# A fused sigmoid-attention and SiLU-MLP kernel rewritten: attention of four heads in 64x64 quadrants, the second matmul by seven products of halves, all engines in one planned order

## The chip, the cores and the metric

The kernel runs on one core of one Trainium2 chip. The metric is the device time of one execution in microseconds (us). Before the change it was 448.87 us, the median of 2 runs (448.57 to 449.17). The span that a profile shows, from the first to the last instruction, is about 2 us shorter than the time of the same run. A *granted clock* is the share of full speed that the matrix engine's clock had in a stretch, as the trace records it. PSUM is the memory into which the matrix engine writes its sums, in banks; SBUF is the memory that holds the operands. DVE, ACT and POOL are VectorE, ScalarE and GpSimd, PE is the matrix engine.

## The reference, cut to what matters

```python
batch, n_heads, seq, head_dim = (8, 12, 448, 64)          # q, k, v, float32
n_tokens, d_model, d_ff = (3584, 768, 2048)               # 3584 = 8 * 448, 768 = 12 * 64

def _attn_ref(q, k, v):
    scores = np.matmul(q, k.transpose(0, 1, 3, 2)) / np.sqrt(64) - np.log(448)
    return np.matmul(1.0 / (1.0 + np.exp(-scores)), v)    # a sigmoid, no row sums

def _moe_ref(x, w_in, w_out):                             # x: heads side by side, 3584 x 768
    h = x @ w_in                                          # "first GEMM"
    return (h / (1.0 + np.exp(-h))) @ w_out               # "second GEMM"
```

## The kernel before

Scores are computed transposed, for a pair of heads at a time, 112 keys per step. Two matmuls, one per head, use the upper and the lower half of the array's rows. The value products use the left and the right half of its columns. ScalarE applies the sigmoid as it empties PSUM.

```python
    def scores(b, hp, c0, c1):
        # ... (tiles)
        for c in range(c0, c1):                           # 4 chunks of 112 keys
            psc = ps_sc.tile([P, 2, 512], F32, ...)
            for j in range(2):                            # 2 heads: 64 rows of the array each
                nc.tensor.matmul(psc[:CP, j, :S],
                    kT[j * D : (j + 1) * D, gi * NCH + c, :],
                    qT[j * D : (j + 1) * D, gi * NCH : (gi + 1) * NCH, :], start=True, stop=True)
            nc.scalar.activation(attnT[:, :, c, :], psc[:CP, :, :S], AF.Sigmoid, ...)

    def values(b, hp):
        # ...
        for c in range(NCH):
            for j in range(2):                            # 2 heads: 64 columns of the array each
                nc.tensor.matmul(pav[j * D : (j + 1) * D, :S],
                    v16[:, 2 * hp + j, c, :], attnT[:, j, c, :], ...)

    def gemm_stream():                                    # both GEMMs, cut into pieces
        for m in range(B // 2):
            for b in (2 * m, 2 * m + 1):
                for fc in range(NFC):                     # first GEMM: 6 matmuls of 448 columns
                    h_unit(b, fc)
                    yield T_H
            for g in range(2 * S // P):
                # ...
                for nh in range(2):
                    for fc in range(NFC):                 # second GEMM: 16 matmuls of 384 columns
                        nc.tensor.matmul(po[:, :NO2], gTs[m][:, fc, g * P : (g + 1) * P],
                                         w_out_sb[:, fc, nh * NO2 : (nh + 1) * NO2], ...)
                # ... scale on VectorE, store
```

Batch 0 runs its attention alone. From batch 1 on, pieces of attention ("visits") are put between pieces of the GEMMs. Of batches 1 to 7, q and k are cast on GpSimd and transposed by DMA; batch 0's are transposed on the matrix engine. Only the instruction orders of the matrix engine (PE) and of GpSimd (POOL) are fixed by hand.

## Time and profile before

| what | number |
|---|---|
| time | 448.87 us |
| PE busy, share of the span | 408.7 us, 91% |
| VectorE (DVE) busy | 173.9 us, 39% |
| ScalarE (ACT) busy | 246.1 us, 55% |
| first matmul of the second GEMM | 118.3 us |

The page of the kernel before, its busy totals and then busy tenths, granted PE clock and DMA share in 40 slices of 11.2 us:

```profile
PE 408.7 (91%) x2480; PEld 197.4 (44%) x2480; DVE 173.9 (39%) x251; ACT 246.1 (55%) x322; POOL 66.3 (15%) x113
...
PE   0477839999999999999999999999999999999996
...
PEclk9998959999999999999999999999999999999999
DMA  9999999999991994089214932071011010000211
```

After about seven slices PE is full to the end. Before that it is not, and there the DMA row is full (it stays full for five slices more). So there are two regimes: a start that waits for data, then a long stretch in which only PE time counts.

The price of PE work is read from the timeline of the kernel before (columns: start, length, engine, line, operation, output<-inputs, shape, count):

```profile
201.61 1.30 PE L201 MATMUL ph_6_1897<-xT_1363,w_in_sb 128*128 128x448 f16 x6
202.84 0.40 PE L161 MATMUL psc_1_2_1907<-qT_0_1280,kT_0_1285 64*112 64x448 f16 x2
203.07 0.35 PE L161 MATMUL psc_1_3_1911<-qT_0_1280,kT_0_1285 64*112 64x448 f16 x2
203.35 1.31 PE L201 MATMUL ph_7_1915<-xT_1363,w_in_sb 128*128 128x448 f16 x6
204.50 1.30 PE L201 MATMUL ph_8_1925<-xT_1363,w_in_sb 128*128 128x448 f16 x6
```

Read starts, not lengths: the lengths of 1.30 us overlap starts that are 1.15 us apart, because matmuls are pipelined. Groups of six without a visit are 1.14 to 1.15 us apart, 0.19 us per matmul; with a visit of two score steps they are 1.74 us apart. The visit costs 0.60 us, of which the two steps are 0.38 and changing to attention's tiling and back is 0.22. Groups of 16 second-GEMM matmuls start 2.60 us apart, 0.1625 us each.

### The profile page before, as it was taken

To read this page: it belongs to the slowest core of one execution; us is meant where nothing else is said; L and a number is where in the kernel's file an instruction comes from. 1 tells how busy PE (TensorE), PEld (TensorE's weight loads), DVE (VectorE), ACT (ScalarE), POOL (GpSimd) and SP (SyncE) were. 2 spreads that over 40 slices of the span, in tenths; PEclk is the share of its full clock that TensorE was granted. 3 is DMA by queue.
4 is the path that set the end of the run, shared out by engine and by line. 5 is a ranking of instruction groups with operands and counts; after the bars stand their busy time and mean duration, and the time that the engine had idled before them with its cause. 6 is when DMAs were issued, how large, how long until landed. Compare 5 with 4: busy or idle time off the path is not lost.

```text
span 447.5 us, 6131 instructions
## 1 busy us (share of the span) xinstructions
PE 408.7 (91%) x2480; PEld 197.4 (44%) x2480; DVE 173.9 (39%) x251; ACT 246.1 (55%) x322; POOL 66.3 (15%) x113
## 2 busy tenths in 40 slices
PE   0477839999999999999999999999999999999996
PEld 0122314344455554444455544444554544455663
DVE  1133314546423235465432335555423235553221
ACT  1356918977644447787545547777555457542000
POOL 1236123262101500051004200130000000000000
PEclk9998959999999999999999999999999999999999
DMA  9999999999991994089214932071011010000211
GB/s 204 221 184 202 244 167 245 264 170 210 202 279 56 214 244 117 1 133 258 42 70 81 285 105 58 2 109 36 5 67 72 35 72 1 0 1 17 90 72 71
DMA packets 81468, 54.86 MB, mean 123 GB/s; under 512 B 40480, under 2 KB 77856, under 8 KB 81440
## 3 DMA queue, kind: packets, MB, share of 16 engines
q1 hardware_dynamic: 65312, 42.67, 40.6%
q0 software_dynamic: 16128, 11.80, 18.5%
q8 instruction: 19, 0.31, 0.3%
q14 instruction: 9, 0.07, 0.0%
HBM read 45.61 MB, written 11.01 MB: 127 GB/s over the span
## 4 chain that ended last, share of the span: by engine, by line
PE 72%; DMA 5%; POOL 1%; DVE 0%; issue 0%
DMA w_out_sb<-in_moe_w_out_dram 5%; PE po_6_1_3490 L228 1%; PE po_5_1_3425 L228 1%; PE po_4_1_3360 L228 1%; PE po_3_1_3302 L228 1%; PE po_3_0_3276 L228 1%; PE po_2_1_3237 L228 1%; PE po_0_1_3093 L228 1%; PE po_0_0_3075 L228 1%; PE po_6_0_2482 L228 1%; PE po_5_0_2403 L228 1%; PE po_4_0_2337 L228 1%; PE po_3_1_2309 L228 1%; PE po_2_0_2210 L228 1%; PE po_1_1_2171 L228 1%; PE po_1_0_2145 L228 1%
## 5 line engine op out<-in xcount | busy, mean ns | idle before, releaser
L201 PEld LDWEIGHTS <-w_in_sb 128*128 128x128 f16 x768 | 71.3, 98 | 79.8 <-issue 19.1
L228 PEld LDWEIGHTS <-gTr_436 128*128 128x128 f16 x224 | 20.9, 98 | 17.8 <-issue 4.9
L228 PEld LDWEIGHTS <-gTr_1537 128*128 128x128 f16 x224 | 20.9, 98 | 17.2 <-issue 4.2
L228 PEld LDWEIGHTS <-gTr_2538 128*128 128x128 f16 x224 | 20.9, 98 | 17.1 <-issue 4.2
L228 PEld LDWEIGHTS <-gTr_3517 128*128 128x128 f16 x224 | 21.9, 98 | 14.5
L131 PE MATMUL ptr_0_k<-ident,x1k_0_109 112*128 112x112 f16 x4 | 0.6, 291 | 11.2 <-POOL x1k_0_109 L125 11.2
L168 ACT ACTIVATE attnT_0_117<-psc_0_0_118,bias_s 112x896 f16<-112x896 f32 x1 | 1.0, 1008 | 15.3 <-PE psc_0_0_118 L161 15.3
L180 PE MATMUL pav_0_485<-attnT_0_427,v_1_399 112*64 112x448 f16 x8 | 1.7, 581 | 7.4 <-DMA v_1_399<-in_v_dram 7.4
L180 PEld LDWEIGHTS <-v_1_399 112*64 112x64 f16 x48 | 2.4, 117 | 10.1 <-DMA v_1_399<-in_v_dram 7.7
L143 POOL DMA_DIRECT2D v_5_1778<-in_v_dram x1 | 0.9, 939 | 36.1 <-PE pav_5_1789 L180 36.1
L143 POOL DMA_DIRECT2D v_6_2279<-in_v_dram x1 | 0.9, 935 | 35.5 <-PE pav_5_2290 L180 35.5
L143 POOL DMA_DIRECT2D v_7_2769<-in_v_dram x1 | 0.9, 935 | 35.0 <-PE pav_5_2780 L180 35.0
L209 ACT ACTIVATE tsig_3_502<-ph_3_495 128x448 f16<-128x448 f32 x1 | 0.5, 544 | 9.7 <-PE ph_3_495 L201 9.7
L180 PEld LDWEIGHTS <-v_0_86 112*64 112x64 f16 x48 | 3.0, 142 | 5.7 <-issue 5.4
L131 PEld LDWEIGHTS <-x1k_0_109 112*128 112x128 f16 x4 | 0.3, 129 | 11.4 <-POOL x1k_0_109 L125 11.4
L188 DVE TENSOR_SCALAR xT_484<-pav_0_485 128x448 f16<-128x448 f32 x1 | 1.1, 1150 | 8.5 <-PE pav_0_485 L180 8.5
L131 PE MATMUL ptr_0_q<-ident,x1q_0_100 112*128 112x112 f16 x4 | 0.6, 294 | 4.1 <-DVE x1q_0_100 L125 4.1
L143 POOL DMA_DIRECT2D v_4_1287<-in_v_dram x1 | 1.0, 955 | 21.2 <-PE pav_5_1298 L180 21.2
L180 PEld LDWEIGHTS <-v_7_2769 112*64 112x64 f16 x48 | 2.2, 109 | 3.0 <-issue 2.1
L180 PEld LDWEIGHTS <-v_3_783 112*64 112x64 f16 x48 | 2.2, 109 | 2.9 <-issue 2.0
L180 PEld LDWEIGHTS <-v_5_1778 112*64 112x64 f16 x48 | 2.2, 109 | 2.9 <-issue 2.0
L180 PEld LDWEIGHTS <-v_2_425 112*64 112x64 f16 x48 | 2.2, 109 | 2.9 <-issue 2.0
(1101 smaller groups left out, 983.6 us busy)
## 6 DMA issues: line engine op xcount, KB each, us to landing
w_in_sb<-in_moe_w_in_dram POOLq DMA_DIRECT2D x4, 768.0 KB, 11.0
w_out_sb<-in_moe_w_out_dram POOLq DMA_DIRECT2D x4, 768.0 KB, 15.6
v_0_86<-in_v_dram POOLq DMA_DIRECT2D x1, 672.0 KB, 12.9
v_1_399<-in_v_dram POOLq DMA_DIRECT2D x1, 672.0 KB, 19.7
v_2_425<-in_v_dram POOLq DMA_DIRECT2D x1, 672.0 KB, 14.9
v_3_783<-in_v_dram POOLq DMA_DIRECT2D x1, 672.0 KB, 7.1
v_4_1287<-in_v_dram POOLq DMA_DIRECT2D x1, 672.0 KB, 7.9
v_5_1778<-in_v_dram POOLq DMA_DIRECT2D x1, 672.0 KB, 7.3
```

Of the source, the lines that this page charges most:

```text
L131: nc.tensor.transpose(ptr[:, c * CP : (c + 1) * CP], x1[:, c].rearrange("p j d -> p (j d)"), ident[:CP, :CP],)
L143: nc.gpsimd.dma_start(v16.rearrange("p h c d -> p h (c d)"), v[b].rearrange("h (p c) d -> p h (c d)", c=NCH),)
L168: nc.scalar.activation(attnT[:, :, c, :], psc[:CP, :, :S], AF.Sigmoid, bias=bias_s[:CP], scale=QKSCALE)
L180: nc.tensor.matmul(pav[j * D : (j + 1) * D, :S], v16[:, 2 * hp + j, c, :], attnT[:, j, c, :], start=(c == 0), stop=(c == NCH - 1),)
L188: nc.vector.tensor_scalar_mul(xTs[b][:, hp, :].rearrange("e (p c) -> e c p", c=NCH), pav[:, :S].rearrange("e (c p) -> e c p", c=NCH), SX,)
L201: nc.tensor.matmul(ph[:, :S], w_in_sb[:, cc, fc * P : (fc + 1) * P], xTs[b][:, cc, :], start=(cc == 0), stop=(cc == NCC - 1),)
L209: nc.scalar.activation(tsig, ph[:, :S], AF.Sigmoid, bias=0.0, scale=ISX)
L228: nc.tensor.matmul(po[:, :NO2], gTs[m][:, fc, g * P : (g + 1) * P], w_out_sb[:, fc, nh * NO2 : (nh + 1) * NO2], start=(fc == 0), stop=(fc ...
```

## The change

The intent is to shorten PE's time. Four heads are handled at once: a score step is four 64x64 matmuls, one in each quadrant of the array, over 64 keys; a value step likewise. The second GEMM takes a pair of 128-token blocks as a 2x2 problem (token blocks by inner halves, times inner halves by output halves) and computes its four results with seven products instead of eight, in the Strassen-Winograd scheme. Four sums of the weights are made once, four sums of activations for each pair, both on DVE (one of each four overwrites an operand). Partial results are accumulated in PSUM, and DVE adds saved copies on the way out. A small model of the engines, run while the program is built, puts all engines' instructions in one fixed order.

The diff replaces nearly everything; its core, cuts marked:

```diff
+class Plan:                       # a model of the engines with assumed durations; it only
+    ...                           # decides the order in which instructions are emitted
-    ctx.enter_context(tc.manual_schedule(engines={mybir.EngineType.PE, mybir.EngineType.Pool}))
+    ctx.enter_context(tc.manual_schedule())
@@ attention: four heads of 64x64
+            for h in range(2):
+                for j in range(2):
+                    nc.tensor.matmul(pt[64 * h : 64 * h + 64, j, :S],
+                        kT[64 * j : 64 * j + 64, s, 64 * h : 64 * h + 64],
+                        qT[64 * j : 64 * j + 64, :, 64 * h : 64 * h + 64], start=True, stop=True)
+    ... (values: 7 chunks x 4 matmuls into one PSUM slot, directly after the group's scores)
@@ loads: one group of four heads ahead; both weights first on the GpSimd queue
+    AHEAD = 1
+    NST = 2                       # staging buffers for q and for k
@@ second GEMM: X, Y, Z are PSUM banks; ra, rb, rc are SBUF copies
+        sums("DVE", ..., [s[:, i] for i in range(3)], a11, a12, a21, a22, "L", prio=-1)
+        prod(1, X, a11, b11, True, ...)
+        pl.op("ACT", ..., nc.scalar.activation(ra, X[:, :HE], AF.Copy, scale=ISX))
+        prod(6, Y, s2, t2, True, ...)
+        comb(rb, Y, ra, kk("u2"), ...)                        # u2 = p1 + p6
+        prod(5, Z, s1, t1, True, ...)
+        prod(2, X, a12, b21, False, ...)                      # c11 = p1 + p2
+        prod(7, Y, s3, t3, False, [kk("u2")] + ...)           # Y = p6 + p7
+        comb(rc, Y, ra, kk("u3"), ...)                        # u3 = p1 + p6 + p7
+        comb(o2[:, HE:], Z, rc, kk("c22"), ...)               # c22 = u3 + p5
+        prod(4, Y, a22, t4, False, [kk("u3")])                # adds onto Y: u3 must have read it
+        comb(o2[:, :HE], Y, ra, kk("c21"), ...)
+        prod(3, Z, s4, b22, False, [kk("c22")] + ...)
+        comb(o1[:, HE:], Z, rb, kk("c12"), ...)
+    ... (visits to attention may fall between products and in the middle of one)
+    plan = [("1", 0), ("1", 1), ("2", 0), ("2", 1), ("2", 2), ("1", 2), ("2", 3), ("2", 4), ...]
```

## The prediction

> **What bounds the kernel now.** The matrix engine, in two regimes. From 120 us on it is never idle: the windows show PE busy 39.5 to 40.0 us in every 40, and the timeline gives one first-GEMM matmul (448 columns) per 0.19 us, one second-GEMM matmul (384 columns) per 0.1625 us (2.60 us per 16 in the chain of waits). Before that it starves: in the first 80 us PE is busy 46.9 us, partly at a granted clock of 0.80 to 0.86, with the DMA share at 1.0 to 1.3 and k's first cast stuck behind the weight gate until 15.2 us. Sum: first GEMM 768 x 0.19 = 146, second 896 x 0.1625 = 146, attention 384 pair steps x 0.19 = 73, 84 visits to attention at about 0.23 us of switching = 20, tail 4. That is 389, so about 60 us are startup.
>
> The switch cost comes from the timeline: a visit with two score steps lengthens the GEMM's group spacing from 1.14 to 1.74 us, 0.22 us more than its two steps. The Trainium skill, "TensorEngine Tiling (Array Packing)", Tiling Modes, says that changing the tiling mode drains the array; the trace agrees, about 0.11 us per change.
>
> **What changes (estimates from those durations).**
> 1. Second GEMM by seven products of halves: 14 x 7 x 8 = 784 matmuls instead of 896: -18 us of PE.
> 2. Four 64x64 quadrants: 336 steps of four matmuls instead of 384 of two. If a step stays at 0.19 to 0.21 us, 64 to 71 us instead of 73: -2 to -9. Four weight loads of 64 columns must fit one step, and may set it.
> 3. ScalarE: 168 sigmoids at the same 0.89 us spacing (896 columns) instead of 192: attention of the first two batches, ScalarE-bound, takes 18.8 instead of 21.4 us each.
> 4. Visits: the planned order has 73 after batch 1, about 0.23 us each = 17.
> 5. Start: no weight gate, one group of four heads transposed at a time, 1792-byte instead of 1024-byte q, k, v packets. But the weights share the DMA with batch 0's q and k. I expect first scores near 11 us and the first GEMM near 37 us. Batch 1's attention is planned wholly after the first GEMM of batch 0, not inside it: about 22 us, ScalarE-bound.
> 6. New waits on PE: product 4 adds onto the bank that the combination after product 7 must first read (about 0.85 us x 14, half filled by visits: 6); operand sums on DVE after the last silu of a first-GEMM block (about 2 us x 6, partly filled: 8).
>
> **Sum.** 37 + 22 + 146 + 127 + attention of six batches 51 + visits 17 + new waits 10 (some overlap) + tail 4 = 414. 1, 2, 4 and 6 lie on the critical path (PE); 3 only in the first two batches.
>
> Predicted 413 us, 80% range 397 to 434; faster by over 2%: 0.92, within 2%: 0.06, slower: 0.02.
>
> **What would show it.** Second-GEMM matmuls still 0.1625 us apart in unbroken runs; quadrant steps of 0.19 to 0.21 us; first first-GEMM matmul at 33 to 42 us; short PE idles released by DVE before products 4 and 6; ScalarE total near 235 us.
>
> **What would make it wrong.** Quadrant matmuls limited by weight loads (0.25 us per step: +15). DMA late in the first 100 us (weights, batch 1 and 2, DMA transposes of 9.5 us of engine time per batch), while the fixed PE order cannot go round a late group: +10 to +25. DVE combinations queueing behind silu products: +10. Fewer stalls and a faster start: -12.

## The result, and the profile after

The changed kernel takes 436.1 us (435.98 and 436.22, 2 runs). The ratio is 0.9704, with a 95% interval of 0.9655 to 0.9753. A ratio here is the mean time of one kernel's runs over the mean of the other's of the same rounds, so not quite the ratio of the quoted medians. Executions over 1.5% slower than the fastest of the same kernel are left out of the means. It is faster, as predicted, but by 12.8 us instead of 36, and outside the predicted range of 397 to 434.

The page of the changed kernel:

```profile
PE 385.4 (89%) x2938; PEld 187.2 (43%) x2938; DVE 195.0 (45%) x298; ACT 224.1 (52%) x326; POOL 69.9 (16%) x92
...
PE   2768977799997999899999999989999999899894
...
PEclk9856985699998999999999999999999999999999
DMA  8999987797257898718881388717820220031022
```

PE is busy 23 us less, yet the time fell by only 13. The PE row shows where the rest went: 8s stand where 9s stood. Of the kernel before, the windows from 160 to 400 us each have PE busy 40.00 of 40 us. Two of them, and then the same two of the changed kernel:

```profile
200.00:240.00 40.00, 40.00 (x252) 19.52 (x252) 16.09 (x23) 23.91 (x32) 2.34 (x4) 1.00 0.50 121
...
360.00:400.00 40.00, 40.00 (x233) 19.11 (x232) 21.14 (x31) 24.27 (x37) 0.00 (x0) 1.00 0.04 15
```

```profile
200.00:240.00 40.00, 38.28 (x292) 18.52 (x291) 17.64 (x28) 22.59 (x35) 7.59 (x9) 1.00 0.66 139
...
360.00:400.00 40.00, 37.26 (x212) 20.29 (x210) 20.56 (x34) 10.95 (x21) 0.00 (x0) 1.00 0.15 41
```

(Columns: window, its length, busy us of PE, weight loads, DVE, ACT and POOL, then clock, DMA share, GB/s.)

The waits of the changed kernel say for what PE waited (total us, times, longest):

```profile
PE gm L653 <- DVE uc L664: 8.4, 12, 1.0
PE gm L653 <- DVE gs L250: 7.5, 7, 1.5
...
PE att L388 <- DMA kT<-xk: 2.4, 1, 2.4
```

Both of the large ones stand inside the seven products. The timeline of the changed kernel shows one of each, in the first pair after a first-GEMM block:

```profile
367.63 1.46 PE L653 MATMUL gm<-wo,gt 128*128 128x384 f16 x8
...
368.41 0.62 DVE L502 TENSOR_TENSOR gt<-gm,sg 128x448 f16<-128x448 f32 x1 [0.51 <-ACT sg L496]
369.07 0.69 DVE L250 TENSOR_TENSOR gs<-gt 128x1024 f16<-128x1024 f16 x1
...
369.80 0.69 DVE L250 TENSOR_TENSOR gs<-gs,gt 128x1024 f16<-128x1024 f16 x1
...
370.54 2.77 PE L653 MATMUL gm<-so,gs 128*128 128x384 f16 x16 [1.45 <-DVE gs L250]
...
373.15 2.76 PE L653 MATMUL gm<-wo,gt 128*128 128x384 f16 x16
...
375.95 0.56 DVE L664 SCALAR_TENSOR_TENSOR uc<-gm,ua 128x384 f32<-128x384 f32 x1 [3.27 <-PE gm L653]
...
376.57 1.46 PE L653 MATMUL gm<-so,gt 128*128 128x384 f16 x8 [0.65 <-DVE uc L664]
```

Product 1 starts at 367.63. Product 6 needs two sums of activations, which cannot start before the last SiLU product (368.41), so it starts at 370.54, 1.6 us late. Later products 2 and 7 run back to back from 373.15 (16 matmuls), and product 4 must wait until DVE has read Y into `uc`: 0.8 us late by the starts. DVE is 45% busy over the span. The lines fit a PE that waits for DVE's latency and not for its throughput; e6 below tests that.

I use one more number below, called **excess spacing**. For each second-GEMM matmul that is followed by another, I take the distance of their starts in the trace minus 0.1625 us, and add these up from 110 us to the end. It was 1.1 us before (from 85 us on) and is 21.6 us after. The seven products remove 112 matmuls of 0.1625 us, 18.2 us.

The third wait above is short but has company. The chain of waits of the changed kernel, in order of time:

```profile
121.24 0.57 DVE ob L664
121.83 0.56 SPq L615
122.44 0.58 SPq L615
123.06 0.58 SPq L204
123.70 6.55 DMA stk<-in_k_dram
130.39 0.95 POOL xk L292
131.52 5.25 DMA kT<-xk
137.19 3.74 PE gm L653 x12
```

A load of k is issued behind two output stores. From its issue it takes 13 us through load, cast and DMA transpose, and PE waits 2.4 us at the end. Then the granted clock is 0.5 from 137.3 to 140.7 us; twelve second-GEMM matmuls took 3.74 us instead of 1.95.

At the start, the first GEMM began at 39.9 us (before: 50.6) and the second at 109.5 us (before: 118.3). The POOL timeline shows why batch 1's attention could not run inside the first GEMM's first block:

```profile
35.19 0.74 POOL L242 DMA_DIRECT2D wo<-in_moe_w_out_dram  x1 [0.27 <-DMA wi<-in_moe_w_in_dram]
35.93 0.94 POOL L292 CAST xq<-stq 128x896 f16<-128x896 f32 x1
36.81 0.94 POOL L292 CAST xk<-stk 128x896 f16<-128x896 f32 x1
50.51 0.94 POOL L292 CAST xq<-stq 128x896 f16<-128x896 f32 x1 [12.76 <-DMA qT<-xq]
57.86 0.94 POOL L292 CAST xk<-stk 128x896 f16<-128x896 f32 x1 [6.42 <-DMA kT<-xk]
```

Batch 1's first casts stand in the queue behind every weight load, until 35.9 us. Their transposes then landed at 50.4 and 57.7 us, 13 and 19 us after issue, while the second weight's 6.3 MB were coming in.

### The profile page after: what moved, and what is told of

It reads as the page before. It is cut to its first block, busy times and chain, and to the rows that moved or that the text cites. A ratio compares the mean times of both kernels' runs of the same rounds, so it can differ in the third digit from the quotient of the medians.

```text
span 434.4 us, 7192 instructions
## 1 busy us (share of the span) xinstructions
PE 385.4 (89%) x2938; PEld 187.2 (43%) x2938; DVE 195.0 (45%) x298; ACT 224.1 (52%) x326; POOL 69.9 (16%) x92
## 4 chain that ended last, share of the span: by engine, by line
PE 78%; DVE 9%; ACT 5%; DMA 4%; issue 1%; SPq 1%; POOL 0%; DVEq 0%; POOLq 0%
PE gm L516 34%; PE gm L653 27%; PE att L406 9%; PE att L388 7%; ACT at L398 5%; DVE gs L250 3%; DVE xt L418 3%; DMA stq<-in_q_dram 2%; DVE uc L664 2%; DMA stk<-in_k_dram 2%; DMA kT<-xk 1%; PE gm L315 1%; DVE ob L664 1%; ACT sg L496 0%; SPq L204 0%
## 5 line engine op out<-in xcount | busy, mean ns | idle before, releaser
L398 ACT ACTIVATE at<-att 128x896 f16<-128x896 f32 x168 | 145.0, 917 | 92.1 <-PE att L388 92.1
L516 PE MATMUL gm<-xt,wi 128*128 128x448 f16 x768 | 151.8, 355 | 0.0
L502 DVE TENSOR_TENSOR gt<-gm,sg 128x448 f16<-128x448 f32 x128 | 79.7, 624 | 79.2 <-ACT sg L496 78.9
L496 ACT ACTIVATE sg<-gm 128x448 f16<-128x448 f32 x128 | 70.0, 547 | 74.4 <-PE gm L516 67.1
L516 PEld LDWEIGHTS <-wi 128*128 128x128 f16 x768 | 73.4, 98 | 76.4 <-issue 12.0
L388 PE MATMUL att<-qT,kT 64*64 64x448 f16 x672 | 57.8, 394 | 18.5 <-ACT at L398 9.8
L653 PEld LDWEIGHTS <-gt 128*128 128x128 f16 x448 | 41.3, 98 | 47.8 <-issue 24.0
L653 PE MATMUL gm<-wo,gt 128*128 128x384 f16 x336 | 61.2, 327 | 0.0
L653 PE MATMUL gm<-so,gs 128*128 128x384 f16 x224 | 40.6, 327 | 7.7 <-DVE gs L250 7.5
L653 PEld LDWEIGHTS <-gs 128*128 128x128 f16 x336 | 31.0, 98 | 35.9 <-DVE gs L250 12.3
L406 PE MATMUL att<-at,v 64*64 64x448 f16 x672 | 43.5, 403 | 1.6 <-ACT at L398 1.6
```

Source lines behind the costliest of these rows:

```text
L388: nc.tensor.matmul(pt[64 * h : 64 * h + 64, j, :S], kT[64 * j : 64 * j + 64, s, 64 * h : 64 * h + 64], qT[64 * j : 64 * j + 64, :, 64 * h ...
L398: lambda: nc.scalar.activation(av[:, :, s, :], pt[:, :, :S], AF.Sigmoid, bias=NEG_LOG_S, scale=QKSCALE),
L406: nc.tensor.matmul(pt[64 * j : 64 * j + 64, h, :S], v16[b % NV][64 * h : 64 * h + 64, 2 * g + j, c * D : (c + 1) * D], av[64 * h : 64 * h ...
L496: lambda: nc.scalar.activation(t, src, AF.Sigmoid, scale=ISX),
L502: lambda: nc.vector.tensor_tensor(o, src.rearrange("p (a t) -> p a t", t=cn), t.rearrange("p (a t) -> p a t", t=cn), ALU.mult),
L516: nc.tensor.matmul(bank[:, :S], wi[:, cc, fc * P : (fc + 1) * P], x[:, cc, :], start=(cc == 0), stop=(cc == NCC - 1),)
```

## The experiments

Theory A: the seven products pay for themselves in PE waits for DVE results, because of the order of products and the sharing of a PSUM bank. Theory B: in the first two batches the order of value products makes ScalarE idle. Theory C: batch 1's data are late because the weight loads stand before them. Theory D: one group of prefetch is too short. The rivals are that DVE is simply short of time, that DMA bandwidth is the limit, or that removing one wait uncovers the next. All runs gave correct results. All were timed against the kernel before in 3 rounds, with 4 runs of each new kernel and 7 of the kernel before; the runs of e1 to e4 shared a chip, and so did those of e5 to e8 and those of e9 and e10.

| run | what | median us | ratio to before (95% interval) |
|---|---|---|---|
| (the change) | | 436.10 | 0.9704 (0.9655 to 0.9753) |
| e1_swap | product 7 before product 2 | 431.26 | 0.9576 (0.9532 to 0.9620) |
| e2_plain | eight plain products | 436.03 | 0.9692 (0.9659 to 0.9725) |
| e3_vlag | value products later | 438.00 | 0.9724 (0.9702 to 0.9746) |
| e4_wolate | second weight loaded later | 430.24 | 0.9568 (0.9501 to 0.9635) |
| e5_ahead | e1 and two groups ahead | 419.65 | 0.9340 (0.9313 to 0.9366) |
| e6_bank4 | product 4 in its own bank | 419.96 | 0.9346 (0.9316 to 0.9376) |
| e7_all | e6, two ahead, weight later | 406.88 | 0.9056 (0.9019 to 0.9092) |
| e8_plain_ahead | e2 and two ahead | 429.69 | 0.9560 (0.9529 to 0.9591) |
| e9_all_vlag | e7 and e3 | 414.45 | 0.9216 (0.9171 to 0.9261) |
| e10_plain_all | e7 with eight products | 421.91 | 0.9384 (0.9338 to 0.9431) |

### e2_plain: undo the seven products

```diff
-        sums_wo(a)
...
-            g2_fast(i, gap)
+            g2_plain(i, gap)     # per 128 tokens and output half: 16 matmuls into one bank,
+                                 # one DVE scaling out; no sums of weights or activations
```

> The seven products are undone: eight products' worth of plain accumulation (896 matmuls of 384 columns), no operand sums on weights or activations, evacuation by one VectorE scaling per half; quadrants, order of blocks and visits as in the changed kernel. Theory A (the seven products save 18.2 us of matmuls and give all of it back in waits for VectorE: 21.6 us of excess spacing inside the second GEMM): time 430 to 436 us, no slower than the changed kernel, excess spacing inside the second GEMM under 2 us. Rival (the waits would stand elsewhere anyway): about 18 us slower, 450 us or more.

It took 436.03 us, the changed kernel 436.10 (ratios to before of 0.9692 and 0.9704, taken in different rounds). The plain kernel issues 112 more matmuls and is no slower. Its excess spacing is 2.1 us, against 21.6. The rival's 450 us is out. As the change was written, the seven products were worth nothing: 18.2 us of matmuls went, and 19.5 us of excess spacing (21.6 minus 2.1) came.

### e1_swap: take away one of the two waits

```diff
+        prod(7, Y, s3, t3, False, [kk("u2")] + sk[:3])
+        comb(rc, Y, ra, kk("u3"), ...)
+        comb(o2[:, HE:], Z, rc, kk("c22"), ...)
         prod(2, X, a12, b21, False, [kk("a")])
-        prod(7, Y, s3, t3, False, [kk("u2")] + sk[:3])
-        comb(rc, Y, ra, kk("u3"), ...)
-        comb(o2[:, HE:], Z, rc, kk("c22"), ...)
         prod(4, Y, a22, t4, False, [kk("u3")])
```

> One edit to the changed kernel: product 7 is issued before product 2, so that product 2 (another bank, 1.3 us) stands between product 7 and product 4. Theory A (the matrix engine waits for the combination that reads the bank of products 6, 7 and 4): the 11 to 12 gaps of 0.8 to 1.1 us before product 4 vanish from the second GEMM's spacing, sum about 9.5 us, time 426 to 428 us. Rival (VectorE is short of time and the wait only moves to another place): time stays above 433 us.

It took 431.26 us, between the two expectations. The waits of e1_swap:

```profile
PE att L388 <- DMA kT<-xk: 7.5, 4, 2.9
PE gm L653 <- DVE gs L250: 6.9, 7, 1.4
```

The wait for `uc` is gone from the list, and excess spacing fell from 21.6 to 10.9 us. So that wait was what theory A says it was. But the wait for a transposed k rose from one of 2.4 us to four, 7.5 us together. PE reached its next score step sooner, and the data were not there. That is theory D, and the rival of the next wait uncovered is right for half of the gain.

### e5_ahead: prefetch two groups instead of one

```diff
-    AHEAD = 1
-    NST = 2
+    AHEAD = 2
+    NST = 3
-    ua = [sb(f"ua{i}", [S], F32) for i in range(2)]     # ub, uc likewise: 448 columns, 384 used
+    ua = [sb(f"ua{i}", [HE], F32) for i in range(2)]    # makes room for the third staging buffer
```

> The kernel of e1_swap with q and k loaded two groups ahead instead of one (three staging buffers instead of two; the three work buffers of the second GEMM are shortened to 384 columns to make room). Theory D (half of what e1_swap won came back as score steps that waited 1.2 to 3.2 us for a transposed k, because load, cast and transpose of one group take about as long as a group's attention slot): the waits between value and score matmuls after 110 us fall from 10.5 to under 6 us, time 424 to 427 us. Rival (that wait is DMA bandwidth, not the distance): no change, 430 us or more.

It took 419.65 us, better than expected. The waits of e5_ahead:

```profile
PE gm L653 <- DVE gs L250: 6.9, 7, 1.4
...
PE att L388 <- DMA kT<-xk: 1.3, 1, 1.3
```

The excess between value and score matmuls (from the start of the last value matmul to that of the next score matmul, less 0.0475 us, a quarter of a step, summed over 16 places after 110 us) fell from 10.5 in e1 to 2.1 us. These 2.1 us are the 0.18 us that an unhindered change takes each time, less the quarter: no wait of this kind is left. Two further gains had not been counted: the granted clock stays at 1.0 from 85.9 us to 417 us (no low-clock stretch after a wait), and the first GEMM starts at 38.5 instead of 40.6 us. The rival's 430 us is out: DMA bandwidth was not the limit; the distance was.

### e6_bank4: take away both waits

```diff
+        iw, W = take()                                   # a fourth bank
         prod(1, X, a11, b11, True, ...)
+        prod(4, W, a22, t4, True, ...)                   # needs no activation sum
         prod(6, Y, s2, t2, True, ...)
         prod(5, Z, s1, t1, True, ...)
+        prod(7, Y, s3, t3, False, [kk("u2")] + ...)      # moved before product 2, as in e1
         prod(2, X, a12, b21, False, [kk("a")])
-        ...                                              # product 7 here, then product 4 on Y
+        comb(o2[:, :HE], W, rc, kk("c21"), ...)          # c21 = u3 + p4
         prod(3, Z, s4, b22, False, [kk("c22")] + ...)
```

> The changed kernel with the seven products in the order 1, 4, 6, 5, 7, 2, 3 and product 4 in a PSUM bank of its own: two products that need no activation sums come first, and another product stands between each combination's source and the next product on its bank. Theory A: excess spacing inside the second GEMM falls from 21.6 to under 5 us; if nothing else held the kernel, 418 us; since e1_swap got back only half, 425 to 429 us with larger waits of score steps for k. Rival (VectorE short of time): excess stays above 12 us, 431 us or more.

It took 419.96 us, better than expected. Excess spacing fell from 21.6 to 2.6 us. The timeline of e6_bank4, at the place that was shown for the changed kernel:

```profile
367.65 1.46 PE L653 MATMUL gm<-wo,gt 128*128 128x384 f16 x8
368.95 1.46 PE L653 MATMUL gm<-so,gt 128*128 128x384 f16 x8
370.25 2.76 PE L653 MATMUL gm<-so,gs 128*128 128x384 f16 x16
372.85 2.76 PE L653 MATMUL gm<-wo,gt 128*128 128x384 f16 x16
```

Eight matmuls per 1.30 us throughout: no product waits. DVE does the same number of sums and combinations as before, so its throughput was not the limit; the rival of a VectorE short of time falls. The wait for k is still there (three times, 5.3 us), as in e1.

### e8_plain_ahead: a control for e5

> Control: e2_plain (eight products, plain accumulation) with q and k two groups ahead. Theory: only the waits of score steps for k go, 430 to 434 us. Compared with e5_ahead it tells what the seven products are worth once product 4 no longer waits: theory A says 5 to 9 us in favour of seven products; the rival says none.

Its edit is that of e2 with that of e5. It took 429.69 us, 10.0 us more than e5_ahead in the same rounds. With one of its two waits removed, the seven products are worth 10 us.

### e4_wolate: load the second weight later

```diff
         pl.op(
-            "POOL", 600, ("wo", h, a), [],
+            "POOL", 600, ("wo", h, a), [("cast", "k", 4)],
```

> One edit: the loads of the second weight are planned on the GpSimd queue after the casts of batch 1's second group, instead of before all of batch 1's casts. Theory C (batch 1's data were late, transposes landing 13 and 20 us after their issue at the same time as 6.3 MB of weights, so that batch 1's attention could not be planned inside the first GEMM of batch 0): two thirds of batch 1's attention now run inside that block; the second block of the first GEMM starts near 76 to 80 us instead of 85, time 427 to 431 us. Rival (loading it later starves the second GEMM): its first matmul does not come earlier than 109 us, time 434 us or more.

It took 430.24 us, inside the expectation. Batch 1's first transposes landed at 39.2 and 40.1 us instead of 50.4 and 57.7, and two of its three groups ran inside the first GEMM's first block. The second block began at 81.6 us, not at the expected 76 to 80: the third group's k was transposed only at 73.4 us, because its load and its transpose now met the weight's. The second GEMM was not starved; it began at 106.1 instead of 109.5 us. Theory C holds.

### e3_vlag: delay the value products

```diff
-        order.append(steps[i])
+        if stp[0] == "V" and not (stp[1] == 0 and stp[2] == NQ - 1) and ...:   # a value step
+            late.append(stp)
+            continue
+        order.append(stp)
+        if stp[0] == "S" and stp[3] == 1:          # after the next group's second score step
+            order += late
+            late = []
+    ... (a batch counts as done only when its late value step is done too)
```

> One edit to the changed kernel: the value products of a group are planned after the second score step of the next group instead of directly after their own last score step (batch 0's last group excepted). Theory B (in the two batches that ScalarE bounds, ScalarE idles about 3 us at each group boundary because the score steps stand behind 28 value matmuls at a low clock): four boundaries shorten by 1.5 to 2.5 us each, time 428 to 431 us. Rival (these stages wait for DMA, not for the order): first GEMM start and end of batch 1's attention unchanged, time 435 us or more.

It took 438.00 us: theory B's gain did not come. Two losses are seen in the trace. The third group of batch 0 waited 1.9 us for its cast on DVE, which the plan had put behind a later scaling, and in batch 1 a score step waited 2.6 us for a transposed k with the value products now behind it. The edit also puts batch 2's first two score steps before the second block of the first GEMM, which began at 90.3 us instead of 84.9. So it changes more than the order inside the two batches, and is no clean test of theory B.

### e9_all_vlag: the same with early data

> e7_all with the late value products of e3_vlag. In e3_vlag that edit cost 2 us, with one score step waiting 2.6 us for a transposed k and the third group's cast held behind a later scaling. If theory B holds once the data are early (ScalarE idles at group boundaries because of the order), batch 1's attention ends 2 to 4 us earlier and the time is 402 to 405 us. Rival (the order of these steps is not what costs, or the later stage loses what the earlier wins): 406 us or more.

It took 414.45 us, 7.6 us slower than e7_all by the medians. The edit lets a batch's last value products wait for the next batch's first score steps. The timeline of e9_all_vlag:

```profile
82.17 0.96 PE L393 MATMUL att<-qT,kT 64*64 64x448 f16 x8 [4.76 <-DMA kT<-xk]
...
86.61 1.87 PE L521 MATMUL gm<-xt,wi 128*128 128x448 f16 x6
```

The second block of the first GEMM began at 86.6 us (e7_all: 76.5), held up by batch 2's k, which it does not need. Even batch 0 was not shorter: its values ended at 38.4 us, against 37.0. So theory B got no support from either run, but as both also made the GEMM block wait for the next batch, they don't refute it. How much of ScalarE's idle time between groups can be won in the first two batches stays open.

### e7_all and e10_plain_all: the sum, and its control

e7_all is e6 with AHEAD = 2, NST = 3 and the second weight's loads after `("cast", "k", 5)`.

> e6_bank4 with q and k two groups ahead and the second weight's loads after the casts of all of batch 1. If theories A, C and D name the three losses, their sum is about 18 + 6 + 8 us less than the changed kernel, some of it shared: 412 to 420 us. If they only move the same wait, above 425 us.

It took 406.88 us, faster than expected, and the fastest of all: 0.9056 of the kernel before. Its page and windows:

```profile
PE 375.4 (93%) x2938; PEld 184.9 (46%) x2938; DVE 194.4 (48%) x298; ACT 223.3 (55%) x326; POOL 71.7 (18%) x92
...
96.00:200.00 104.00, 103.97 (x898) 49.73 (x896) 49.47 (x77) 69.72 (x98) 20.45 (x24) 1.00 0.74 160
200.00:300.00 100.00, 98.48 (x828) 46.93 (x826) 49.32 (x76) 64.54 (x96) 17.72 (x20) 1.00 0.64 138
300.00:400.00 100.00, 99.16 (x640) 53.17 (x636) 54.18 (x89) 35.34 (x58) 0.00 (x0) 1.00 0.17 42
```

From 96 to 400 us PE is idle 2.4 of 304 us. The second GEMM begins at 95.9 us.

> Control for e7_all: the same kernel with eight plain products instead of seven. With the waits gone the seven products should be worth nearly their 112 matmuls of 0.1625 us: theory A says 421 to 425 us, that is 14 to 18 us slower than e7_all. Rival (operand sums and combinations cost the matrix engine something even so): under 10 us slower, below 417 us.

The control took 421.91 us, 15.0 us more than e7_all by the medians, which are of different rounds (ratios of 0.9384 and 0.9056, a difference of 0.033 of some 449 us). With the waits gone the seven products give 15 of the 18.2 us that counting matmuls promises. In the profiled runs most of the rest is found: excess spacing of 1.5 us against 0.6, and 1.8 us more for e7_all's visits, one of which waited 1.5 us at 217.7 us for DVE to empty an attention bank.

## Why the prediction was right or wrong

The sum in the prediction was 414 us. The span was 434.4 us and the time 1.7 us more.

**Right: the mechanism and the prices.** Second-GEMM matmuls stayed 0.1625 us apart in unbroken runs, and six first-GEMM matmuls 1.14 us. A quadrant step took 0.19 us: a visit of two score steps again lengthens the spacing by 0.60 us (groups of twelve that start at 87.23 and 90.11 us, minus 12 x 0.19). ScalarE was busy 224 us (predicted near 235). By the same reading, attention costs PE 10.6 us per batch (for each group of four heads three visits of 0.60 and one of 1.74) against 12.5 (for each pair of heads 1.48 and 0.60). Over six batches that is about 11 us, inside the 5 to 12 us that items 2 and 4 of the prediction add up to. The first GEMM began at 39.9 us, inside the 33 to 42 that was given.

**Wrong: item 6, "New waits on PE", 14 us before and 10 after an allowance for overlap.** The kinds, the places and the numbers were right: 12 late starts of product 4 and 7 late sums, against 14 and 6. The size was not. Adding the late starts in the trace, the wait before product 4 came to about 10.3 us (predicted 6) and the wait for sums to about 8.6 (predicted 8). I had let visits fill half of the former. They filled it in 2 of 14 cases. Five of the other twelve stand after the last attention matmul (344.8 us), where no visit is left to fill them; in the other seven the plan made none; by the kernel's code it makes one only when its own clock, its pause of 1.5 us between visits and the step's inputs allow it. The further allowance of 4 us for overlap had no basis. Measured: 19 us against 10.

**Wrong: item 1 as a gain of its own.** The prediction booked -18 us for seven products as work on the critical path and the waits as a smaller, separate item. e2 shows that they cancel (436.03 against 436.10 us), and e10 that 15 us appear once the order of the products hides the DVE results.

**Not in the sum: late data.** "DMA late", with +10 to +25, stood among the things that could make it wrong, and the fixed order could indeed not go round a late group. In the changed kernel it cost the chain 2.4 us of waiting and about 1.8 us of low clock at 137 us, and it kept batch 1's attention out of the first GEMM's block; e4 (-5.9 us) and e5 (-11.6 us on top of e1) show what was to be won there, both by medians of different rounds.

**Too small: batch 1's attention alone.** Predicted 22 us, measured 25.8 (59.1 to 84.9 us). ScalarE's part was even less than the 18.8 us: 21 sigmoids 0.81 us apart are 17.0. The change from one group of heads to the next cost more than was booked:

```profile
64.61 2.83 PE L406 MATMUL att<-at,v 64*64 64x448 f16 x28 [0.22 <-ACT at L398]
67.18 0.64 PE L388 MATMUL att<-qT,kT 64*64 64x448 f16 x4
68.70 0.96 PE L388 MATMUL att<-qT,kT 64*64 64x448 f16 x8 [0.89 <-DVE xt L418]
```

PE ran at a granted clock of 0.64 between 60 and 80 us, though none of its waits there was longer than 1.1 us. The 28 value matmuls of a group took about 2.6 us instead of 1.4, and the second score step of the next group waited 0.9 to 1.1 us for DVE to empty the bank of the values. ScalarE had little to do meanwhile. No run separates the low clock from the order. The first block of the first GEMM also took 1.0 us more than its 18.2.

The terms: start +2.9, first block +1.0, batch 1's attention +3.8, new waits +9, late data +4, a tail of 5.7 us from the start of the last matmul instead of 4, and attention about 3 less than booked. That is about +20, of 20.4 between the sum and the span.

The prediction's use of the Trainium skill, "TensorEngine Tiling (Array Packing)", Tiling Modes (a change of tiling mode drains the array), was borne out: 0.09 us into attention (0.28 us from the last first-GEMM matmul to the first score step instead of 0.19) and about 0.10 us out of it, before and after. With 0.02 to 0.04 us more for the first step, that is the 0.22. Its Restrictions section also says that column tiling disables fast weight load. That fits the trace of the changed kernel: from 110 us on, loads of 64 columns took about 106 ns, no less than the 98 of full 128-column ones. With four of them per step the 0.19 us held, so they did not set the pace.

One wait for sums has a further part: at 181.84 us a sum took 1.30 us instead of 0.68 while a GpSimd cast ran beside it, and that wait of PE was the longest of its kind (1.70 us by the starts). The Trainium skill, "SBUF — State Buffer", states under "Who interferes with whom" that a DVE operation with two SBUF inputs and a GpSimd operation that reads SBUF exclude each other on a shared port. The trace agrees with that in this place; no run tested it.

## What to carry to other kernels

An algorithm with fewer products saves PE time only as far as PE does not wait for the extra work on the other engines. What helped here: start with the products that need no sums, and put an independent product, or another bank, between each product that must be read and the next one on its bank. An engine at 45% busy can still hold up PE by its latency, so count the waits in the chain and not the busy share. In a planned order each wait that is removed brings the next data need forward: here prefetch had to grow to cover the 13 us chain of load, cast and transpose (e5), and large loads that were needed late must not stand in a queue before small ones that were needed soon (e4).

## What the Trainium skill lacked or had wrong

- "TensorE: Matmul & The Clock Gate": idle gaps of more than about 3 us bring back the low clock (section "Why this matters for your kernels"). Here a wait of 2.4 us at 134 to 137 us was followed by a granted clock of 0.5 from 137.3 to 140.7 us (12 matmuls in 3.74 us instead of 1.95). A wait of 2.4 us at 131 to 133 us in e4_wolate was not followed by one.
- "TensorEngine Tiling (Array Packing)", Tiling Modes: it says that a change of mode drains the array but gives no time. Here it is 0.09 us into 64x64 and about 0.10 us back. A change from score to value matmuls cost 0.09 us in the kernel before (two tilings: 0.28 us between starts instead of 0.19); from value to score matmuls in the changed kernel (one tiling) it cost nothing (0.18 us).
- "DMA: Bandwidth & Descriptors": I found no statement of how many loads from the GpSimd queue may be outstanding before its next issue blocks the engine. Here there were never more than eight in the first 36 us of the changed kernel: from the ninth to the twenty-fifth load each was issued 0.28 to 0.29 us after the load eight before it had landed. GpSimd was held up from 7.1 us on, 3.4 us the longest, and the casts behind the loads until 35.9 us. Whether the chip or the program's semaphores set the eight, no run shows.
- No page that I read treats products of halves summed in PSUM. Here seven products were worth 0 us with exposed waits (e2), 10.0 with one of them hidden (e8 against e5), and 15.0 with both hidden (e10 against e7).
